# Weight pieces of 1024 elements in place of 512 for the later experts, and tokens taken counted in one column

## The chip, the cores and the metric

The kernel runs on one core of one Trainium2 chip. The core has a matrix engine (PE; PEld is its weight load), a vector engine (DVE), a scalar engine (ACT), a general engine (POOL) and a queue engine (SP) that issues most transfers. Each engine works through its own instructions in order and waits on semaphores for the others. The metric is the time of one execution in microseconds (us); three runs of the kernel before give the median.

## The reference

A sparse attention feeds a mixture of experts in which each expert has a fixed number of places:

```python
scores = scale * np.matmul(q, k.transpose(0, 1, 3, 2))     # 8 batches, 8 heads, 576 positions, 64 wide
masks = ...                                                # 4 heads local, 4 heads strided, stride 32
attn = exp(scores - max) / sum
x = (attn @ v) as (N, D) = (4608, 512)

cap = N // E                                               # 4608 / 8 = 576
logits = x @ w_gate
order = np.argsort(-flat)                                  # all (token, expert) pairs, best first
for idx in order:
    tok, e = (int(idx) // E, int(idx) % E)
    if assigned[tok] >= 0 or counts[e] >= cap:
        continue
    assigned[tok] = e
    counts[e] += 1
for e in range(E):
    mask = assigned == e
    h = np.maximum(x[mask] @ w1[e], 0.0)                   # w1[e]: 512 x 1024
    out[mask] = h @ w2[e]                                  # w2[e]: 1024 x 512
```

The assignment is greedy over all pairs, so the experts fill up one after the other: the first to fill is the one whose 576th best token has the highest logit, and so on.

## The kernel before

The first third of the span is attention, which writes the tokens to a scratch in HBM and leaves the logits in `L` (128 partitions x 36 columns of tokens x 8 experts). Then come eight phases (`ph`, called expert 0 to 7 here, in the order in which they fill up).

For each phase a *search* finds the threshold at which the next expert is full: six rounds, each with `cm` on DVE (L824, compares every token's best logit with 32 candidates), nine counting matmuls on PE (L840), `red` and `r` on DVE (L843, L846), a folding matmul (L849), `g` on DVE (L856 or L853), a spreading matmul (L859) and the next candidates `cand` (L862). `slots` numbers the chosen tokens (DVE and one pair of matmuls), `close` sets the filled expert's logits to a large negative number and finds every token's new best expert (`point`), `take` removes the chosen tokens, `indices` and `tokens` make the token list and gather the tokens. `ffn` does the expert's matmuls: `hidden` (L1159, x times w1, evacuated by ACT at L1166 and DVE at L1167) and the second product (L1207, L1201), stored at L1218.

Everything of float32 precision goes through PE as two float16 parts. `weights` fetches a phase's w1 and w2 (eight transfers on SP), squares them on ACT (`square`, L1002, four pieces of 1024 columns) to find a power of two as scale (`scale`, a matmul at L1010 and four small DVE instructions), and then cuts them: `split` writes `hi` = float16 of w times scale on ACT (L1020) and `lo` = the rest on DVE (L1021). `parts` says into which pieces: w1 (4 chunks x 1024 columns) into eight pieces of 4 x 128 columns, w2 (8 chunks x 512) into eight pieces of one chunk, each 512 elements in a partition.

PE's order is written out by hand from first to last (the generators yield a cost for each matmul, and the chain that is due next gets its turn); its matmuls for the search stand in fixed places between those of `ffn`. In phase 0 ACT's order is by hand as well. The order of the other engines comes from a planner that puts instructions into the order of their planned starts; work of the search and the evacuations is marked urgent, the pieces of the weights are not. `spread` hands the pieces over with due times (`T_SQ`, `T_SCALE`, `T_CUT`, 1500 each, after `T_W` of 4000), all at once when the phase that needs them has begun. So the search, its DVE work and the cutting of the next expert's weights run beside the matmuls of the present expert. The weights in float32 have one buffer (`wp`), hi and lo have two (`w16`).

`take` (L931) makes `pen`, a large negative number for each token taken, adds it to the tokens' best logits `rm`, and gives back a function that adds it to all eight logits of the token in `L`; the next search calls that function in its first round (`more`, L834).

Of the kernel before, what the change touches and what calls it, by code (L numbers as in the profile page):

```python
# [8 lines left out]
F32 = mybir.dt.float32  # L9
# [4 lines left out]
OP = mybir.AluOpType  # L14
# [5 lines left out]
N, DM, E, FF = B * S, H * D, 8, 1024  # L20
CAP = N // E
# [16 lines left out]
BIG = 1.0e30  # L38
J1, R1, GC = 32, 6, 4
J0, JL, R0, CUTS0 = 32, 16, 6, (16, 12, 8)  # L40
TP = 128
NC = N // TP
# [13 lines left out]
T_F, T_LOAD0, T_HOT1, T_W, T_SQ, T_SCALE, T_CUT, T_BULK0 = 3000, 1500, 6350, 4000, 1500, 1500, 1500, 600  # L56
# [76 lines left out]
def band_stride_attention_then_capacity_moe(ctx, tc, qt, kl, ks, nl, ns, wg, w1, w2, cst, out, dbg=None):  # L133
    nc = tc.nc
# [46 lines left out]
    L = const.tile([TP, NC, E], F32, name="L")  # L181
# [38 lines left out]
    with tc.tile_pool(name="ld", bufs=2) as ld, \  # L220
# [44 lines left out]
        class Unit:  # L265
# [71 lines left out]
            def room(u, p):  # L337
                u.sp[p] = ps_a.tile([128, 2, BANK], F32, name="spa")
# [133 lines left out]
        parts = (range(4, LT), range(4))  # L472
# [53 lines left out]
        todo = [Unit(b, strided) for b in range(B) for strided in (True, False)]  # L526
# [53 lines left out]
        def pair(i):  # L580
            return (todo[i // 2], i % 2) if 0 <= i <= last else None
# [27 lines left out]
        for i in range(-1, 2 * nu):  # L609
            u, n, m = pair(i), pair(i + 1), pair(i + 2)  # L610
# [7 lines left out]
            if m or i in mids:  # L618
                a = room(m) if m else ps_a.tile([128, 2, 512], F32, name="spa")
            if i in mids or i in mids2 or i in mids3:  # L620
                b = ps_b.tile([128, 512], F32, name="spb")
# [81 lines left out]
    rt = ctx.enter_context(tc.tile_pool(name="rt", bufs=2))  # L703
    r1 = ctx.enter_context(tc.tile_pool(name="r1", bufs=1))
# [28 lines left out]
                                       op1=OP.add)  # L733

    HV = 32
    rvb = [r1.tile([TP, HV, NC], F16, name=f"rv{i}") for i in range(2)]
    for t in rvb:
        nc.gpsimd.memset(t[:, 3 * SHI:], 0.0)
# [5 lines left out]
    def urgent(ph=1):  # L744
        return tc.high_priority(offset=URGENT * (2 if ph == 0 else 1))
# [183 lines left out]
            *point(slice(0, NC), rm, ohc, wmc)]  # L929

    def take(slot, rm):  # L931
        pen = rt.tile([TP, NC], F32, name="pen")
        nc.vector.tensor_scalar(pen, slot, CAP - 0.5, -BIG, op0=OP.is_lt, op1=OP.mult)
        nc.vector.tensor_tensor(rm, rm, pen, op=OP.add)
        return lambda: nc.vector.tensor_tensor(L, L, pen[:, :, None].to_broadcast([TP, NC, E]), op=OP.add)

    def indices(ph, slot):
        hurry = ph in HURRY
# [20 lines left out]
        with urgent(ph):  # L959
            pi = ps_r.tile([128, 512], F32, name="pr_")  # L960
            for c in range(NC):
                g = c % 4
                nc.tensor.matmul(pi[HV * g:HV * g + HV, :SLO], rv[:, :, c], ohl[c // nh][:, :, c % nh], start=(c < 4),
                                 stop=(c >= NC - 4), skip_group_check=True)
# [13 lines left out]
    def weights(ph, ei):  # L978
        e = nc.sync.value_load(ei[0:1, 0:1], min_val=0, max_val=E - 1)
        res, todo = [], []  # L980
        for name, w, nch, width, bits in (("w1", w1, DC, FF, W1_BITS), ("w2", w2, FC, DM, W2_BITS)):
            wf = wp.tile([128, nch, width], F32, name=name)
            src = w[bass.ds(e, 1)].rearrange("o (c p) f -> p (o c) f", p=128)
            n4 = nch // 4
            def fetch_w(cs, wf=wf, src=src, n4=n4):
                for c in cs:
                    nc.sync.dma_start(wf[:, c * n4:c * n4 + n4], src[:, c * n4:c * n4 + n4])  # L987

            k = W_EARLY if ph == 0 and name == "w2" else 4
            fetch_w(range(k))  # L990
            if k < 4:
                def later(wf=wf, k=k, n4=n4, go=fetch_w):
                    nc.gpsimd.memset(wf[:, k * n4:, :1], 0.0)
                    go(range(k, 4))
            sq = rt.tile([128, 4], F32, name="sq")
            sc = rt.tile([128, 2], I32, name="w_s" + name)
            hi = w16.tile([128, nch, width], F16, name=name + "h")
            lo = w16.tile([128, nch, width], F16, name=name + "l")

            def square(c, wf=wf, sq=sq, n4=n4):  # L1000
                jk = r1.tile([128, 1024], F16, name="jk")
                nc.scalar.activation(jk, wf[:, c * n4:(c + 1) * n4].rearrange("p c f -> p (c f)"), AF.Square,  # L1002
                                     scale=1.41422, accum_out=sq[:, c:c + 1])

            def scale(sq=sq, sc=sc, bits=bits):
                ss = rt.tile([128, 1], BF16, name="ss")
                with nc.allow_low_precision(reason="only the power of two of the sum is used, with a factor of two to spare"):
                    nc.vector.tensor_reduce(ss, sq, axis=AX.X, op=OP.add)
                pt = ps_r.tile([128, 512], F32, name="pr_")
                nc.tensor.matmul(pt[:, :1], ones_b, ss, start=True, stop=True)  # L1010
                scale_of(pt[:, :1], bits, rt, sc)

            def parts(nch=nch, width=width):
                if nch == DC:
                    return [(slice(0, nch), slice(k, k + 128)) for k in range(0, width, 128)]
                return [(slice(k, k + 1), slice(0, width)) for k in range(nch)]

            def split(c, f, k, wf=wf, sc=sc, hi=hi, lo=lo):
                s_ = sc.bitcast(F32)[:, 0:1]
                nc.scalar.activation(hi[:, c, f], wf[:, c, f], AF.Copy, scale=s_)  # L1020
                nc.vector.scalar_tensor_tensor(lo[:, c, f], wf[:, c, f], s_, hi[:, c, f], op0=OP.mult,  # L1021
                                               op1=OP.subtract)

            todo.append([(T_SQ, lambda c=c, g=square: g(c)) for c in range(4)])
            todo.append([(T_SCALE, scale)])
            todo.append([(T_CUT, lambda c=c, f=f, k=k, g=split: g(c, f, k)) for k, (c, f) in enumerate(parts())])
            res += [hi, lo, sc.bitcast(F32)]
        sq1, sc1, cut1, sq2, sc2, cut2 = todo
        if ph == 0:
            with urgent(0):  # L1030
                for _, f in sq1:
                    f()

            def start():
                return lambda: [f() for _, f in sc1]

            def more():
                with urgent(0):
                    for _, f in cut1[:CUT0]:
                        f()  # L1040
                g = spread(ph, cut1[CUT0:])
                chains.append([due_now(), g])
                second.append(slowly([(T_W20, lambda: None)] + sq2 + sc2 + cut2))
                chains.append([due_now(), second[0]])
                return g

            return res, (start, more, later)
        todo = [(T_W, lambda: None)] + sq1 + sc1
        for a, b in zip(cut1[:4], sq2):
            todo += [a, b]  # L1050
        todo += cut1[4:6] + sc2 + cut1[6:] + cut2
        g = spread(ph, todo)
        chains.append([due_now(), g])
        return res, g
# [178 lines left out]
    def due_now():  # L1233
        return clock
# [10 lines left out]
    with tc.manual_schedule(engines=MAN):  # L1245
        work[0] = now[:4] + (now[4](),)
        chains.append([T_LOAD0, load0()])
        for ph in range(E):
            with tc.manual_schedule(engines=MAN0) if ph in MANP else nullcontext():
                while ph not in ready:  # L1250
                    c = min(chains, key=lambda c: c[0])
# [79 lines left out]
```

## Time and profile before

| | us |
|---|---|
| median of 3 runs | 712.11 (708.58 to 715.13) |
| the profiled execution | 713.84 |
| its span, first to last instruction | 712.1 |
| expert 0 starts (first L1159) | 259.2 |
| last matmul of expert 7 | 700.8 |
| mean granted TensorE clock | 0.907 |

The span is the time between the first and the last instruction that the profiler saw; some 1.7 us of the execution lie around it. In the rows of the profile, a name such as `w2l<-w,w_sw,w2h` is what the instruction writes and reads, `128x512` is partitions x elements, and a bracket at the end of a timeline row is the idle time of the engine just before, with the one that ended it. A matmul's own time (some 0.38 us for 512 columns) overlaps the next one's. Groups of lines with the weight pieces: L1020 and L1021, 64 instructions each for w1 and w2, eight for each matrix.

### The profile page before, as it was taken

The numbers are of one execution on the slowest core, as the hardware profiler recorded it, in microseconds if no ns is written. First come the engines' busy times: TensorE is split into PE (matmuls) and PEld (weight loads), VectorE is DVE, ScalarE is ACT, GpSimd is POOL, SyncE is SP. The second block draws the span as 40 slices with busy tenths as digits, with TensorE's granted clock in tenths as the row PEclk, the third lists the DMA queues.
The fourth block names the chain that finished last, engine by engine and source line by source line (L and its number), as shares of the span: only waits on it lengthen the run. The fifth ranks groups of instructions, "written<-read, shape, count | busy, mean of one in ns | idle before, by whom it ended". The sixth has DMA issues, their size and how long they took to land.

```text
span 712.1 us, 19031 instructions
## 1 busy us (share of the span) xinstructions
PE 614.3 (86%) x7974; PEld 392.3 (55%) x7977; DVE 465.3 (65%) x1326; ACT 318.9 (45%) x497; POOL 156.7 (22%) x152
## 2 busy tenths in 40 slices
PE   7778777788984368899989999999999989999993
PEld 4555555566663346546635745745654754755741
DVE  4797656787786788858857877867768543552200
ACT  3635634554521055555544644833823746452210
POOL 2053413323331030050041031211212111402011
PEclk9888978987786579999999999999999999999997
DMA  9999999999642270391671671852652684341010
GB/s 252 265 262 255 248 230 255 239 234 209 167 103 67 68 231 28 135 267 36 237 156 45 238 154 46 276 110 90 229 112 75 237 236 151 90 94 52 2 37 29
DMA packets 111472, 111.24 MB, mean 156 GB/s; under 512 B 76405, under 2 KB 84175, under 8 KB 110876
## 3 DMA queue, kind: packets, MB, share of 16 engines
q1 hardware_dynamic: 103307, 88.49, 47.9%
q0 software_dynamic: 7360, 21.15, 9.5%
q8 instruction: 62, 1.02, 0.6%
q10 hardware_dynamic: 720, 0.39, 0.2%
q14 instruction: 23, 0.18, 0.1%
HBM read 73.63 MB, written 18.87 MB: 130 GB/s over the span
## 4 chain that ended last, share of the span: by engine, by line
PE 26%; issue 12%; DVE 10%; DMA 8%; ACT 3%; POOL 2%; SPq 1%; POOLq 0%; ACTq 0%
PE ph L1207 12%; PE ph L1159 8%; DMA w<-in_w_dram 7%; PE ph L1201 2%; DVE w2l L1021 2%; ACT jk L1002 2%; DVE cm L824 1%; POOL out_dram L1218 1%; DVE hl L1167 1%; SPq L987 1%; DVE w1l L1021 1%; DMA xg<-x_scr,idx 1%; POOL xg L1072 1%; ACT hh L1166 1%; DVE ohl L955 1%
## 5 line engine op out<-in xcount | busy, mean ns | idle before, releaser
L1159 PE MATMUL ph<-xt,w1h 128*128 128x288 f16 (+2 forms) x1024 | 177.5, 287 | 2.0 <-ACT xt L1062 2.0
L1159 PEld LDWEIGHTS <-w1h 128*128 128x128 f16 x1024 | 97.4, 98 | 30.9 <-issue 5.3
L1159 PE MATMUL ph<-xt,w1l 128*128 128x288 f16 (+2 forms) x512 | 111.4, 287 | 0.0
L1218 POOL DMA_INDIRECT out_dram<-y,idx x40 | 44.0, 1100 | 254.4 <-ACT y L1217 229.1
L1207 PE MATMUL ph<-w2l,hh 128*128 128x512 f16 x256 | 97.8, 382 | 2.3 <-DVE w2l L1021 2.3
L1207 PE MATMUL ph<-w2h,hh 128*128 128x512 f16 x256 | 97.9, 382 | 1.9 <-ACT hh L1166 1.9
L1002 ACT ACTIVATE jk<-w 128x1024 f16<-128x1024 f32 x64 | 67.4, 1053 | 71.3 <-DMA w<-in_w_dram 69.8
L1207 PE MATMUL ph<-w2h,hl 128*128 128x512 f16 x256 | 97.8, 382 | 0.2 <-DVE hl L1167 0.2
L1167 DVE SCALAR_TENSOR_TENSOR hl<-ph,hh 128x576 f16<-128x576 f32 (+2 forms) x72 | 49.3, 686 | 53.6 <-ACT hh L1166 53.4
L1207 PEld LDWEIGHTS <-hh 128*128 128x128 f16 x512 | 47.9, 98 | 56.6 <-issue 5.1
L1166 ACT ACTIVATE hh<-ph 128x576 f16<-128x576 f32 (+2 forms) x72 | 42.5, 591 | 79.8 <-PE ph L1159 78.4
L1072 POOL DMA_INDIRECT xg<-x_scr,idx x40 | 43.2, 1080 | 135.5 <-DVE idx L975 100.5
L380 ACT ACTIVATE pr<-spa 128x576 f32<-128x576 f32 x32 | 20.8, 649 | 92.8 <-PE spa L376 83.3
L1217 ACT ACTIVATE y<-ph,so 128x512 f32<-128x512 f32 x32 | 21.9, 685 | 89.5 <-PE ph L1207 79.9
L1159 PEld LDWEIGHTS <-w1l 128*128 128x128 f16 x512 | 49.5, 98 | 14.1 <-issue 2.3
L428 POOL TENSOR_TENSOR xos<-xs,xos 118x768 f16<-118x768 f32 x16 | 27.1, 1694 | 113.4 <-ACT xos L427 113.4
L1021 DVE SCALAR_TENSOR_TENSOR w1l<-w,w_sw,w1h 128x512 f16<-128x512 f32 x64 | 46.1, 743 | 2.4 <-ACT w1h L1020 1.6
L1021 DVE SCALAR_TENSOR_TENSOR w2l<-w,w_sw,w2h 128x512 f16<-128x512 f32 x64 | 45.8, 743 | 1.7 <-ACT w2h L1020 1.6
L397 PE MATMUL po<-v_s,pr 64*54 64x65 f32 (+1 forms) x768 | 41.3, 259 | 5.3 <-issue 3.8
L1020 ACT ACTIVATE w1h<-w,w_sw 128x512 f16<-128x512 f32 x64 | 41.6, 711 | 8.4 <-DVE g L856 3.7
L1020 ACT ACTIVATE w2h<-w,w_sw 128x512 f16<-128x512 f32 x64 | 41.0, 710 | 5.0 <-DVE w_sw L208 4.9
L1207 PEld LDWEIGHTS <-hl 128*128 128x128 f16 x256 | 25.1, 98 | 30.2 <-issue 3.1
(571 smaller groups left out, 947.2 us busy)
## 6 DMA issues: line engine op xcount, KB each, us to landing
w<-in_w_dram SPq DMA_DIRECT2D x64, 512.0 KB
kl<-in_kl_dram SPq DMA_DIRECT2D x16, 304.0 KB
v_s<-in_ns_dram SPq DMA_DIRECT2D x16, 292.5 KB
v_l<-in_nl_dram SPq DMA_DIRECT2D x16, 292.5 KB
ks<-in_ks_dram SPq DMA_DIRECT2D x16, 288.0 KB
qs<-in_qt_dram SPq DMA_DIRECT2D x16, 288.0 KB
ql<-in_qt_dram SPq DMA_DIRECT2D x16, 288.0 KB
x_scr<-xol SPq DMA_DIRECT2D x8, 512.0 KB
```

What stands on the lines that cost most here:

```text
L397: nc.tensor.matmul(po[r:r + n, j - j0], pr[k, o:o + n], u.vn[k, t, 2 * p + h], start=(j == j0), stop=(j == j1 - 1), skip_group_check=True)
L428: eng.tensor_tensor(u.xo[:nr, :, 1, c], xf, u.xo[:nr, :, 0, c], op=OP.subtract)
L1002: nc.scalar.activation(jk, wf[:, c * n4:(c + 1) * n4].rearrange("p c f -> p (c f)"), AF.Square, scale=1.41422, accum_out=sq[:, c:c + 1])
L1020: nc.scalar.activation(hi[:, c, f], wf[:, c, f], AF.Copy, scale=s_)
L1021: nc.vector.scalar_tensor_tensor(lo[:, c, f], wf[:, c, f], s_, hi[:, c, f], op0=OP.mult, op1=OP.subtract)
L1072: nc.gpsimd.indirect_dma_start(out=xg[:n], out_offset=None, in_=x_rows, in_offset=bass.IndirectOffsetOnAxis(ap=idx[:n, t:t + 1], axis=0))
L1159: nc.tensor.matmul(tile_[:, j, :w], wt[:, d, f * 128:(f + 1) * 128], xt[:, d // 2, xx, d % 2, c], start=(k == 0), stop=(k == 3 * DC - 1))
L1166: nc.scalar.activation(hv, src, AF.Relu)
L1167: nc.vector.scalar_tensor_tensor(lv, src, 0.0, hv, op0=OP.max, op1=OP.subtract)
L1207: nc.tensor.matmul(py, a[:, f, ts_], w[:, f], start=(k == 0), stop=(k == len(todo) - 1))
L1217: nc.scalar.activation(y, py, AF.Copy, scale=so[:, t:t + 1])
L1218: st = nc.gpsimd.indirect_dma_start(out=out_rows, out_offset=bass.IndirectOffsetOnAxis(ap=idx[:n, t:t + 1], axis=0), in_=y[:n], in_offset= ...
```

## The change

Two edits. In `weights`, `parts` makes pieces of twice the size for every phase but 0: w1 in four pieces of 4 x 256 columns, w2 in four pieces of two chunks, each 1024 elements in a partition; the due time of a piece is doubled with it. The list in which squares, scale and cuts follow one another is written anew for that: one cut of w1 ahead of each of the first three squares of w2, then the fourth square and the scale, then the last cut of w1 and those of w2.

In `take`, the tokens taken are counted in a column `taken` (one number for each token, zero at first), and `rm` gets `taken` times the large negative number. `L` is left alone: the function that was given back does nothing. Where `close` makes `rm` anew from `L`, the next `take` marks all tokens taken so far, not only the last ones.

```diff
+    taken = r1.tile([TP, NC], F32, name="taken")
+    nc.gpsimd.memset(taken, 0.0)
...
     def take(slot, rm):
-        pen = rt.tile([TP, NC], F32, name="pen")
-        nc.vector.tensor_scalar(pen, slot, CAP - 0.5, -BIG, op0=OP.is_lt, op1=OP.mult)
-        nc.vector.tensor_tensor(rm, rm, pen, op=OP.add)
-        return lambda: nc.vector.tensor_tensor(L, L, pen[:, :, None].to_broadcast([TP, NC, E]), op=OP.add)
+        nc.vector.scalar_tensor_tensor(taken, slot, CAP - 0.5, taken, op0=OP.is_lt, op1=OP.add)
+        nc.vector.scalar_tensor_tensor(rm, taken, -BIG, rm, op0=OP.mult, op1=OP.add)
+        return lambda: None
...
             def parts(nch=nch, width=width):
+                n = 2 if ph else 1
                 if nch == DC:
-                    return [(slice(0, nch), slice(k, k + 128)) for k in range(0, width, 128)]
-                return [(slice(k, k + 1), slice(0, width)) for k in range(nch)]
+                    return [(slice(0, nch), slice(k, k + 128 * n)) for k in range(0, width, 128 * n)]
+                return [(slice(k, k + n), slice(0, width)) for k in range(0, nch, n)]
...
-            todo.append([(T_CUT, lambda c=c, f=f, k=k, g=split: g(c, f, k)) for k, (c, f) in enumerate(parts())])
+            todo.append([(T_CUT * (2 if ph else 1), lambda c=c, f=f, k=k, g=split: g(c, f, k)) for k, (c, f) in enumerate(parts())])
...
         todo = [(T_W, lambda: None)] + sq1 + sc1
-        for a, b in zip(cut1[:4], sq2):
-            todo += [a, b]
-        todo += cut1[4:6] + sc2 + cut1[6:] + cut2
+        for k, a in enumerate(cut1[:3]):
+            todo += [a, sq2[k]]
+        todo += sq2[3:] + sc2 + cut1[3:] + cut2
```

## The prediction

> **What bounds the kernel now.** I read the page's head first, then the windows cut at the starts of the experts, then who waited for whom on PE, and last the timelines of DVE, ACT and PE around the weight pieces.
>
> ```profile
> span 712.1 us, 19031 instructions
> PE 614.3 (86%) x7974; PEld 392.3 (55%) x7977; DVE 465.3 (65%) x1326; ACT 318.9 (45%) x497; POOL 156.7 (22%) x152
> ```
>
> The windows show experts 1, 4 and 7 (columns: stretch, length, then busy time of PE, PEld, DVE, ACT, POOL, granted clock, DMA).
>
> ```profile
> 324.20:383.60 59.40, 55.79 (x433) 32.55 (x431) 44.95 (x130) 31.76 (x53) 10.75 (x10) 0.97 0.47 131
> ...
> 494.90:551.90 57.00, 53.95 (x422) 32.14 (x421) 42.25 (x133) 27.30 (x45) 11.91 (x10) 1.00 0.48 146
> ...
> 653.60:700.90 47.30, 47.19 (x313) 29.26 (x311) 6.81 (x9) 8.71 (x14) 4.80 (x5) 1.00 0.07 26
> ```
>
> Expert 7 has nothing beside it and takes 47.30 us, PE busy in 47.19: that is the matmul work of one expert. Experts 1 to 4 take 55 to 59 us. What they have more is the search for the next expert's threshold (its matmuls on PE) and stalls of PE. So PE sets the end, and the change touches no PE instruction of any size. ACT (27.30 of 57.00 us in expert 4) has room, DVE (42.25) some. The pieces can only move the time through the waits of PE. These are the ones after the first expert's start that matter (waits: waiter, whom for, us in total, times, longest):
>
> ```profile
> PE ph L1207 <- DVE w2l L1021: 2.3, 1, 2.3
> ...
> PE ph L1207 <- ACT hh L1166: 1.9, 1, 1.9
> PE pr__5641 L849 <- DVE r L846: 1.9, 1, 1.9
> ...
> PE pr__7713 L849 <- DVE red L843: 1.6, 1, 1.6
> ...
> PE pr__7012 L849 <- issue: 1.5, 1, 1.5
> ...
> PE pr__6336 L849 <- issue: 0.7, 1, 0.7
> ```
>
> and, asked of L849 alone, the waits of PE before it that r ended (us, times):
>
> ```profile
>   DVE r L846: 3.0, 5
> ```
>
> L849 is the second PE step of a search round (L840 counts, DVE makes red and r, L849 folds, DVE makes g, L859 spreads, DVE makes cand and cm, L840 again). PE's order is written out by hand, so when r is late, every matmul of the expert behind L849 waits. The four large L849 waits (1.9, 1.6, 1.5, 0.7) make 5.7 us.
>
> **Pieces of 1024.** For experts 1 to 7 each weight matrix is cut in 4 pairs of instructions (hi on ACT, lo on DVE) where it was 8: 56 pairs fewer in all. The durations:
>
> ```profile
> L1002 ACT ACTIVATE jk<-w 128x1024 f16<-128x1024 f32 x64 | 67.4, 1053 | 71.3 <-DMA w<-in_w_dram 69.8 <-ACT jk L1002 0.3
> ...
> L1021 DVE SCALAR_TENSOR_TENSOR w2l<-w,w_sw,w2h 128x512 f16<-128x512 f32 x64 | 45.8, 743 | 1.7 <-ACT w2h L1020 1.6
> ```
>
> The stretch that I replay is the second matrix of the expert prepared during expert 3, on ACT, DVE and PE:
>
> ```profile
> 479.75 4.40 ACT L1020 ACTIVATE w2h<-w,w_sw 128x512 f16<-128x512 f32 x7 [1.36 <-DVE w_sw L208]
> ```
>
> ```profile
> 480.17 1.36 DVE L824 TENSOR_TENSOR cm<-rmn,cand 128x1152 f16<-128x1152 f32 x1
> 481.44 2.07 DVE L1021 SCALAR_TENSOR_TENSOR w2l<-w,w_sw,w2h 128x512 f16<-128x512 f32 x3
> 483.43 0.18 DVE L843 TENSOR_TENSOR red<-pr__7241,fold 128x32 f16<-128x32 f32 x1
> 483.53 0.74 DVE L1021 SCALAR_TENSOR_TENSOR w2l<-w,w_sw,w2h 128x512 f16<-128x512 f32 x1
> 484.19 0.20 DVE L846 TENSOR_REDUCE r<-red 128x8 f16<-128x32 f16 x1
> ...
> 486.38 0.20 DVE L862 SCALAR_TENSOR_TENSOR cand<-steps,pr__7241,cand 128x1 f32<-128x1 f32 x1
> 486.51 0.73 DVE L1021 SCALAR_TENSOR_TENSOR w2l<-w,w_sw,w2h 128x512 f16<-128x512 f32 x1
> ...
> 487.46 1.34 DVE L824 TENSOR_TENSOR cm<-rml,steps 128x1152 f16<-128x1152 f32 x1
> ```
>
> ```profile
> 482.80 0.38 PE L840 MATMUL pr__7241<-ohn,cm 128*128 128x32 f16 x9
> 484.63 0.18 PE L849 MATMUL pr__7241<-r,fold 128*32 128x8 f16 x1
> 486.14 0.17 PE L859 MATMUL pr__7241<-ih,ones_j 32*128 32x1 f16 x1
> 489.28 0.38 PE L840 MATMUL pr__7309<-ohn,cm 128*128 128x32 f16 x9
> ```
>
> On ACT seven pieces take 4.40 us, 0.63 apiece. A 1024 square takes 1.05, less some 0.09 of overlap with the next (0.71 alone against 0.63 in the train), so 0.96: each merged pair saves 2 x 0.63 - 0.96 = 0.30, over 56 pairs 17 us of ACT time. On DVE three take 2.07, so one more costs 0.67. The nearest long row is cm, 1152 elements in 1.36 alone and 1.27 to the next start (480.17 to 481.44): scaled to 1024 some 1.15 to 1.20. I take 1.20, a saving of 2 x 0.67 - 1.20 = 0.14, 8 us in all. Neither is on the path: ACT idles half the stage, and DVE's weights are ready well ahead (this matrix is done at 487, and the expert that uses it starts at 494.9). So: 0 us.
>
> What is on the path is that DVE does not interrupt a piece. Between red (483.43) and r (484.19) a piece was put into the gap that r waits for red, and another ran into red's start. I replay with 1.20: the hi pieces are ready at 480.8, 481.8, 482.7, 483.7; DVE runs one from 481.44 to 482.64 and one to 483.84, so red starts at 483.84 and not 483.43. A third fills the gap from 483.95 to 485.15, r ends at 485.35, and L849 starts near 485.4 in place of 484.63: 0.8 us of new stall. The fourth ends at 486.47, ahead of L859 at 486.14 + 0.8, so it costs nothing. One matrix pays 0.8 once. Searches run while experts 0 to 4 compute, so ten matrices (two each of experts 1 to 5) meet one. For the five second matrices I take 0.8 each; the five first ones have squares of 1.05 us between their pieces on ACT, so they reach DVE less densely, and I take half: 5 x 0.8 + 5 x 0.4 = 6. From that goes what small pieces cost there now: r ended five waits of 3.0 us in all, and without the 1.9 four are left with 1.1, one of them beside expert 0's own pieces; I take 0.8. Sum **+5.2**. The ends: 0, if the planner keeps the gaps free, less the 0.8; and 1.4 a matrix, +13, if a piece also lands ahead of cand and between cand and cm. That link has 0.5 us of room (cm ends at 487.46 + 1.34 = 488.80, PE takes it at 489.28), and two places at 1.20 - 0.67 = 0.53 each are 1.1, so 0.6 more.
>
> **Stops of DVE that no engine explains.** Three of the four L849 waits follow idle time on DVE before red, although L840 had ended long before:
>
> ```profile
> 364.18 0.19 DVE L843 TENSOR_TENSOR red<-pr__5641,fold 128x32 f16<-128x32 f32 x1 [2.53 <-PE ph L1201]
> ...
> 463.43 0.19 DVE L843 TENSOR_TENSOR red<-pr__7012,fold 128x32 f16<-128x32 f32 x1 [0.94 <-PE ph L1159]
> ...
> 517.60 0.19 DVE L843 TENSOR_TENSOR red<-pr__7713,fold 128x32 f16<-128x32 f32 x1 [1.08 <-PE ph L1159]
> ```
>
> ```profile
> 364.18:412.72 48.54, 38.67 (x114) 1.00 0.48 142
> 412.72:463.43 50.71, 38.37 (x114) 1.00 0.54 160
> 463.43:517.60 54.17, 38.71 (x115) 1.00 0.49 142
> ```
>
> ```profile
> q14 instruction: 23, 0.18, 0.1%
> ```
>
> The stops lie 114 or 115 counted DVE instructions apart (busy instructions of the windows that begin and end at them), as a fixed block of the instruction stream would, and the instruction queue loads 0.18 MB in 23 packets, 8 KB each. My reading is that DVE waits for its next block of instructions, once an expert, each time just before red. The change takes 9 DVE instructions out of each later expert (8 pieces, 1 update of L), so the stops wander off red by 9, 18, 27 places. Where a stop lands outside a search round it costs PE nothing, inside one about as much as now. These three waits are 5.0 us; I take **-2**, ends 0 and -5.0.
> The Trainium skill, page "Runtime: NRT & Kernel Launch", section "Instruction fetch mechanics", says that a sequencer fetches its next block while it runs the present one, so that the crossing is mostly hidden. The idle 2.53, 0.94 and 1.08 us speak against that for DVE. By the page's rule this term would be 0 and the sum 2 us higher.
>
> **Tokens taken.**
>
> ```profile
> 444.18 0.19 DVE L900 SCALAR_TENSOR_TENSOR sc<-df,mine 128x36 f16<-128x36 f32 x1
> ...
> 448.08 0.18 DVE L933 TENSOR_SCALAR pen<-slot 128x36 f32<-128x36 f32 x1
> ...
> 448.29 0.20 DVE L934 TENSOR_TENSOR rmn<-rmn,pen 128x36 f32<-128x36 f32 x1
> 448.41 0.45 DVE L935 TENSOR_TENSOR L<-L,pen 128x288 f32<-128x288 f32 x1
> ```
>
> Two instructions stay two, now both of the kind of L900 (0.19, an upper end of 0.26 for f32 output): +0.1 at most, seven times, in a stretch where PE has other matmuls. Six updates of L of 0.45 go (0.37 each to the next start at 448.78). Only the one late in expert 0 can be on the path: PE waits 2.3 us there for w2l, whose last piece is queued on DVE behind the work on the next expert's tokens: **-0.4**, ends 0 and -2.3 (if the planner also moves that piece ahead). The memset of 36 columns is one more on POOL, which is busy 22% of the span: 0. In the new order of the todo list only ACT squares and the scale of the second matrix change places with cuts; the due times add up as before (28000 to the scale, 43000 to the end), no DMA is moved, and SP's and POOL's queues stay: 0.
>
> **One wait absorbs.** L1207 waits 1.9 us for hh on ACT late in expert 5, where ACT is held by squares that wait for weights from HBM. PE coming later loses that much less: **-0.9**, ends 0 and -1.9.
>
> **Sum.** 5.2 - 2 - 0.4 - 0.9 = +1.9 us. The profiled execution took 713.84 us (span 712.1 and 1.7 around it), 0.2% above the median 712.11. Against it the sum gives 715.7, against the median **714**.
>
> **The rivals.** *Slower.* Every one of the ten matrices pays in both links, 1.4 us: +13 in place of 5.2, sum +9.9, **722 us**. It decides from about 1.1 us a matrix (7.1 us for the 1%, and 3.3 + 0.8 to make up, over ten). For it: the gaps between red and r and between cand and cm are filled with pieces wherever pieces are there. Against: with half as many pieces, a matrix rarely has one for each gap. *Faster.* The planner leaves no long piece in a gap (0 - 0.8), all three stops leave search rounds (-5.0) and the w2l wait goes (-2.3), with 0.7 of the fourth L849 wait: **703 us**. Against: search rounds fill most of each expert's time, so a stop finds another one. *Hidden.* New stalls equal what the stops and the 0.4 give: **712 us**, if only the second matrices pay 0.8 (4 - 0.8 - 2 - 0.4 - 0.9 = 0).
>
> **How the numbers follow.** Forecast 714 (and its surroundings above 712) 0.35, hidden 0.23, slower 0.25, faster 0.17. A time within 1% of 712.11 (705.0 to 719.2) is what a measurement of this kernel can't tell from no change: 0.58 for that, 0.25 above it, 0.17 below. The range 704 to 724 leaves out about half of the faster case and the edge of the slower one.
>
> **What would show it.** L1020 and L1021 rows of 128x1024 x56 and near 0.96 and 1.2 us; DVE's count 62 lower. Right on the main step: L849 and L840 waits on r and cm of 0.3 to 1 us in several rounds of experts 0 to 4, a 1024 piece between red and r. Wrong if those rounds keep their 1.8 us from L840 to L849. Right on the stops: long idle time of DVE without a late releaser, off red and off the places above. If it is still before red in each expert, the block reading is wrong. The prediction as a whole is wrong if PE's waits in experts 5 to 7 or before 255 us change by more than 2 us.

## The result and the profile after

| | before | after |
|---|---|---|
| median of 4 runs each (us) | 713.55 (708.58 to 715.13) | 721.81 (720.62 to 724.61) |
| ratio, 95% interval | 1 | 1.0107 [1.0062, 1.0152] |
| the profiled execution (us) | 713.84 | 722.52 |
| its span (us) | 712.1 | 720.8 |
| mean granted TensorE clock | 0.907 | 0.902 |
| expert 0 starts, expert 7 ends (us) | 259.2, 700.8 | 260.9, 709.6 |

By the ratio the kernel became slower by 1.1%, 7.6 us; the two medians lie 8.3 us apart. The head of the page after:

```profile
span 720.8 us, 18914 instructions
...
PE 619.2 (86%) x7974; PEld 396.1 (55%) x7977; DVE 457.3 (63%) x1264; ACT 308.5 (43%) x441; POOL 166.5 (23%) x153
```

DVE has 62 instructions less and is busy 8.0 us less, ACT 10.4 us less. Two engines do less, and the span is 8.7 us longer: what they save is not on the path, as the prediction had it.

The windows of the profiled kernel after show experts 2, 4, 5 and 7 (columns as in the prediction), and those of the kernel before experts 2 and 5, which the prediction did not show.

```profile
382.40:441.70 59.30, 55.51 (x424) 32.53 (x423) 42.52 (x115) 25.57 (x37) 13.25 (x10) 0.97 0.43 132
499.00:556.50 57.50, 53.98 (x422) 32.03 (x421) 41.06 (x123) 25.69 (x37) 15.07 (x10) 1.00 0.54 145
556.50:613.30 56.80, 51.19 (x355) 30.75 (x354) 22.48 (x52) 32.81 (x51) 13.03 (x10) 0.94 0.69 199
662.30:709.60 47.30, 47.18 (x313) 29.25 (x311) 6.81 (x9) 8.72 (x14) 4.79 (x5) 1.00 0.07 26
```

```profile
383.60:438.50 54.90, 53.91 (x424) 32.22 (x423) 44.39 (x126) 27.10 (x46) 11.42 (x10) 1.00 0.48 142
551.90:604.10 52.20, 49.60 (x356) 30.41 (x355) 23.55 (x60) 31.74 (x55) 9.01 (x9) 1.00 0.66 205
```

The lengths say where to look. Expert 7 is 47.30 us as before; expert 2 is 4.4 us longer and expert 5 4.6 us. Over all eight the gain and loss come to +7.0 us (441.6 to 448.6). The other 1.7 us lie ahead of the experts, where the change has one memset, and where the start moves from run to run in any case: over the traces of all kernels shown here expert 0 starts between 255.8 and 264.8 us.

The waits of PE after (waiter, whom for, us in total, times, longest; most lines are two higher here, so L849 is L851 now, L840 is L842, L1207 is L1209):

```profile
PE ph L1209 <- ACT hh L1168: 5.3, 1, 5.3
...
PE pr__6954 L851 <- DVE r L848: 2.2, 1, 2.2
...
PE pr__6296 L851 <- DVE r L848: 2.1, 1, 2.1
...
PE pr__7637 L851 <- DVE r L848: 1.7, 1, 1.7
...
PE pr__4952 L842 <- DVE cm L826: 1.2, 1, 1.2
...
PE pr__5619 L851 <- DVE r L848: 0.6, 1, 0.6
```

and asked of L851 alone, where the kernel before had five waits of 3.0 us:

```profile
  DVE r L848: 10.8, 11
```

So there are two places: the search (many waits for r, some for cm) and one single wait for hh, 1.9 us before and 5.3 now. The wait for w2l of 2.3 us is gone from the list.

Some waits stand in the profile as "issue", so for comparing kernels I worked the stalls out in one way for all: between the starts of two successive matmuls of PE, less the first one's own 0.12 or 0.21 us, summed where over 0.15 us is left, from the first L1159 on (L1161 after). By it:

| kernel | hi on ACT | lo on DVE | take | ratio to before [95%] | r | cm | hh | w2l | idx, tokens | experts |
|---|---|---|---|---|---|---|---|---|---|---|
| before | 512 | 512 | old | 1 | 8.6 | 2.8 | 2.1 | 2.4 | 7.6 | 441.6 |
| after | 1024 | 1024 | new | 1.0107 [1.0062, 1.0152] | 12.8 | 4.6 | 5.4 | 0 | 6.3 | 448.6 |
| e1 | 1024 | 1024 | old | 1.0187 [1.0129, 1.0245] | 12.9 | 4.6 | 6.5 | 2.4 | 8.8 | 455.7 |
| e2 | 512 | 512 | new | 0.9987 [0.9951, 1.0022] | 9.4 | 3.0 | 3.2 | 0 | 8.0 | 442.1 |
| e3 | 1024 | 512 | new | 0.9907 [0.9868, 0.9947] | 7.1 | 3.3 | 0 | 0 | 8.4 | 435.8 |
| e4 | 512 | 1024 | new | 1.0064 [1.0028, 1.0099] | 13.3 | 4.4 | 2.3 | 0 | 6.3 | 444.6 |
| e5 (after, gap closed) | 1024 | 1024 | new | 1.0018 [0.9979, 1.0056] | 4.5 | 5.6 | 5.7 | 0 | 6.8 | 443.0 |
| e6 (before, gap closed) | 512 | 512 | old | 1.0047 [1.0008, 1.0086] | 3.8 | 4.2 | 4.7 | 2.4 | 10.2 | 445.2 |
| e7 (e3, gap closed) | 1024 | 512 | new | 0.9939 [0.9897, 0.9980] | 3.9 | 5.2 | 0 | 0 | 8.1 | 435.3 |
| e8 (before, 64 more on DVE) | 512 | 512 | old | 1.0000 [0.9952, 1.0047] | 5.0 | 3.4 | 4.3 | 2.4 | 7.8 | 441.8 |
| e9 (after, hh first) | 1024 | 1024 | new | 1.0072 [1.0036, 1.0107] | 13.2 | 5.5 | 0 | 0 | 9.4 | 447.9 |
| e10 (e2, hh first) | 512 | 512 | new | 0.9957 [0.9921, 0.9993] | 7.5 | 3.3 | 0 | 0 | 9.5 | 438.9 |
| e11 (e5, hh first) | 1024 | 1024 | new | 0.9991 [0.9967, 1.0016] | 3.1 | 6.3 | 0 | 0 | 11.0 | 445.9 |
| e12 (e3 again) | 1024 | 512 | new | 0.9943 [0.9899, 0.9987] | 4.7 | 4.7 | 0 | 0 | 8.8 | 435.3 |

The stalls are those of one profiled execution each; the ratios leave out disturbed runs, which the medians given with the experiments still hold. How far two executions differ can be seen from e8, which is the kernel before but for 64 small instructions at its start and takes the same time: r and cm wait 8.4 us there in place of 11.4, hh 4.3 in place of 2.1. A difference of some 3 us in one column between two kernels is therefore no finding by itself. A wait for y on ACT, of 0.6 to 3.5 us in e9 to e12, has no column. From before to after r and cm together grow by 6.0 us, hh by 3.3, w2l goes by 2.4, idx and tokens by 1.3: +5.6 of the +7.0 us of the experts. All stalls together, the small ones too, grow by 6.7 us by the same count; the remaining 0.3 us I do not assign.

Now the same stretch that the prediction replayed (second matrix, prepared during expert 3). The timelines of ACT, DVE and PE after:

```profile
483.08 4.26 ACT L1022 ACTIVATE w2h<-w,w_sw 128x1024 f16<-128x1024 f32 x4 [1.37 <-DVE w_sw L208]
```

```profile
483.50 1.36 DVE L826 TENSOR_TENSOR cm<-rmn,cand 128x1152 f16<-128x1152 f32 x1
484.77 2.47 DVE L1023 SCALAR_TENSOR_TENSOR w2l<-w,w_sw,w2h 128x1024 f16<-128x1024 f32 x2
487.16 0.18 DVE L845 TENSOR_TENSOR red<-pr__7177,fold 128x32 f16<-128x32 f32 x1
487.26 1.28 DVE L1023 SCALAR_TENSOR_TENSOR w2l<-w,w_sw,w2h 128x1024 f16<-128x1024 f32 x1
488.46 0.20 DVE L848 TENSOR_REDUCE r<-red 128x8 f16<-128x32 f16 x1
...
490.42 0.22 DVE L864 SCALAR_TENSOR_TENSOR cand<-steps,pr__7177,cand 128x1 f32<-128x1 f32 x1 [0.35 <-PE pr__7177 L861]
```

```profile
486.13 0.38 PE L842 MATMUL pr__7177<-ohn,cm 128*128 128x32 f16 x9
488.71 0.17 PE L851 MATMUL pr__7177<-r,fold 128*32 128x8 f16 x1 [0.68 <-DVE r L848]
490.21 0.17 PE L861 MATMUL pr__7177<-ih,ones_j 32*128 32x1 f16 x1
```

Two long pieces run ahead of red, a third between red and r, and PE takes r 2.58 us after the start of its counting (486.13 to 488.71), where it was 1.83 (482.80 to 484.63). That is 0.75 us later; the replay had 0.8. The fourth piece ended early enough, as in the replay.

In the three rounds where DVE stood still before red in the kernel before, DVE does not stand still now. This is the second of them, DVE after:

```profile
463.49 2.48 DVE L1023 SCALAR_TENSOR_TENSOR w1l<-w,w_sw,w1h 128x1024 f16<-128x1024 f32 x2
465.88 0.75 DVE L1169 SCALAR_TENSOR_TENSOR hl<-ph,hh 128x576 f16<-128x576 f32 x1
466.54 0.18 DVE L845 TENSOR_TENSOR red<-pr__6954,fold 128x32 f16<-128x32 f32 x1
466.64 1.28 DVE L1023 SCALAR_TENSOR_TENSOR w1l<-w,w_sw,w1h 128x1024 f16<-128x1024 f32 x1
467.83 0.20 DVE L848 TENSOR_REDUCE r<-red 128x8 f16<-128x32 f16 x1
```

The stop is gone, and the wait that PE has for it is larger than before (2.2 in place of 1.5), because long pieces stand ahead of red and behind it. (The tile of this round is `pr__7012` in the kernel before.)

### The profile page after: what moved, and what is told of

Read it like the earlier page. It is cut to its first block, busy times and chain, and to the rows that moved or that the text cites. A ratio compares the mean times of both kernels' runs of the same rounds, so it can differ in the third digit from the quotient of the medians.

```text
span 720.8 us, 18914 instructions
## 1 busy us (share of the span) xinstructions
PE 619.2 (86%) x7974; PEld 396.1 (55%) x7977; DVE 457.3 (63%) x1264; ACT 308.5 (43%) x441; POOL 166.5 (23%) x153
## 4 chain that ended last, share of the span: by engine, by line
PE 23%; issue 17%; DVE 12%; DMA 8%; ACT 3%; POOL 3%; SPq 1%; POOLq 0%; DVEq 0%; ACTq 0%
PE ph L1209 12%; PE ph L1161 7%; DMA w<-in_w_dram 6%; DVE w1l L1023 2%; DVE w2l L1023 2%; PE ph L1203 2%; ACT jk L1003 2%; DVE cm L826 2%; DMA xg<-x_scr,idx 1%; POOL out_dram L1220 1%; DVE hl L1169 1%; POOL xg L1074 1%; SPq L988 1%; ACT hh L1168 0%; ACT w2h L1022 0%
## 5 line engine op out<-in xcount | busy, mean ns | idle before, releaser
L1161 PE MATMUL ph<-xt,w1h 128*128 128x288 f16 (+2 forms) x1024 | 177.9, 288 | 1.1 <-DVE w1l L1023 1.1
L1161 PEld LDWEIGHTS <-w1h 128*128 128x128 f16 x1024 | 97.6, 98 | 30.9 <-issue 5.3
L1161 PE MATMUL ph<-xt,w1l 128*128 128x288 f16 (+2 forms) x512 | 111.5, 288 | 0.0
L1220 POOL DMA_INDIRECT out_dram<-y,idx x40 | 48.8, 1221 | 250.7 <-ACT y L1219 227.2
L1209 PE MATMUL ph<-w2h,hh 128*128 128x512 f16 x256 | 98.0, 383 | 5.3 <-ACT hh L1168 5.3
L1209 PE MATMUL ph<-w2h,hl 128*128 128x512 f16 x256 | 98.1, 383 | 0.0
L1209 PE MATMUL ph<-w2l,hh 128*128 128x512 f16 x256 | 98.0, 383 | 0.0
L1209 PEld LDWEIGHTS <-hh 128*128 128x128 f16 x512 | 47.8, 98 | 62.8 <-issue 6.0
L1074 POOL DMA_INDIRECT xg<-x_scr,idx x40 | 47.5, 1189 | 136.2 <-DVE idx L976 86.9
L1161 PEld LDWEIGHTS <-w1l 128*128 128x128 f16 x512 | 49.5, 98 | 15.1 <-issue 3.3
L1023 DVE SCALAR_TENSOR_TENSOR w1l<-w,w_sw,w1h 128x1024 f16<-128x1024 f32 (+1 forms) x36 | 41.2, 1159 | 3.6 <-ACT w1h L1022 3.6
L1023 DVE SCALAR_TENSOR_TENSOR w2l<-w,w_sw,w2h 128x1024 f16<-128x1024 f32 (+1 forms) x36 | 41.3, 1158 | 2.9 <-ACT w2h L1022 2.8
L826 DVE TENSOR_TENSOR cm<-rmn,cand 128x1152 f16<-128x1152 f32 x30 | 40.7, 1356 | 0.6
L1209 PEld LDWEIGHTS <-hl 128*128 128x128 f16 x256 | 25.1, 98 | 28.6 <-issue 1.3
L397 PEld LDWEIGHTS po<-v_s,pr 64*54 64x54 f32 (+1 forms) x768 | 31.7, 149 | 14.4 <-issue 8.8
```

Source lines behind the costliest of these rows:

```text
L397: nc.tensor.matmul(po[r:r + n, j - j0], pr[k, o:o + n], u.vn[k, t, 2 * p + h], start=(j == j0), stop=(j == j1 - 1), skip_group_check=True)
L826: nc.vector.tensor_tensor(cm, src[:, :, None].to_broadcast([TP, NC, J1]), t[:, None, :].to_broadcast([TP, NC, J1]), op=OP.is_ge)
L1074: nc.gpsimd.indirect_dma_start(out=xg[:n], out_offset=None, in_=x_rows, in_offset=bass.IndirectOffsetOnAxis(ap=idx[:n, t:t + 1], axis=0))
L1161: nc.tensor.matmul(tile_[:, j, :w], wt[:, d, f * 128:(f + 1) * 128], xt[:, d // 2, xx, d % 2, c], start=(k == 0), stop=(k == 3 * DC - 1))
L1209: nc.tensor.matmul(py, a[:, f, ts_], w[:, f], start=(k == 0), stop=(k == len(todo) - 1))
L1220: st = nc.gpsimd.indirect_dma_start(out=out_rows, out_offset=bass.IndirectOffsetOnAxis(ap=idx[:n, t:t + 1], axis=0), in_=y[:n], in_offset= ...
```

## The experiments

**One edit at a time.** e1 has the pieces and the old `take`:

```diff
...
-                    return [(slice(0, nch), slice(k, k + 128)) for k in range(0, width, 128)]
-                return [(slice(k, k + 1), slice(0, width)) for k in range(nch)]
+                    return [(slice(0, nch), slice(k, k + 128 * n)) for k in range(0, width, 128 * n)]
+                return [(slice(k, k + n), slice(0, width)) for k in range(0, nch, n)]
```

> Pieces of 1024 for experts 1 to 7, take as before. Theory (a long DVE piece ahead of the search's red, r or cm makes PE wait): 6 to 9 us over the kernel before, and 8 or 9 of the waits of the folding matmul for r at 0.5 us or more. Rival (the edit of take costs the time): within 2 us of the kernel before.

Measured: 727.98 us beside 717.63 for the kernel before, ratio 1.0187 [1.0129, 1.0245], which is 9.3 to 17.6 us over: more than the 6 to 9 expected. r and cm wait as long as in after (17.5 us together), eight of the waits for r are of 0.5 us or more, and the 2.4 us for w2l are back.

e2 has the new `take` and pieces of 512:

```diff
...
-        nc.vector.tensor_tensor(rm, rm, pen, op=OP.add)
-        return lambda: nc.vector.tensor_tensor(L, L, pen[:, :, None].to_broadcast([TP, NC, E]), op=OP.add)
+        nc.vector.scalar_tensor_tensor(rm, taken, -BIG, rm, op0=OP.mult, op1=OP.add)
+        return lambda: None
```

> Only the edit of take. Theory: within 2 us of the kernel before, rather below (six updates of L of 0.45 us less on DVE, the order of the pieces unchanged). Rival (take costs the time): 4 us or more over the kernel before.

Measured: 0.9987 [0.9951, 1.0022], some 0.9 us below, within the 2 us expected. The edit of `take` does not cause the loss; the pieces do. The w2l wait is gone with the new `take` in all kernels that have it and stands at 2.4 us in all that lack it (before, e1, e6, e8); yet e2 is not faster by that, since hh waits 3.2 in place of 2.1 and r 9.4 in place of 8.6.

**Which of the two halves of a pair.** In e3 and e4 one half of each pair is long and the other short. e3 (hi 1024 on ACT, lo 512 on DVE; `two` gives the two halves of a piece):

```diff
...
-                nc.vector.scalar_tensor_tensor(lo[:, c, f], wf[:, c, f], s_, hi[:, c, f], op0=OP.mult,
-                                               op1=OP.subtract)
+                for a, b in two(c, f):
+                    nc.vector.scalar_tensor_tensor(lo[:, a, b], wf[:, a, b], s_, hi[:, a, b], op0=OP.mult,
+                                                   op1=OP.subtract)
```

> The changed kernel, but each lo piece on DVE cut in two of 512; hi on ACT stays 1024, and the order of squares, scale and cuts is the changed one. Theory (the length on DVE is what costs): within 2 us of the kernel before; waits of L849 for r no larger than before. Rival (the longer ACT pieces, or the new order of the list, hold up hh or the scale): 5 us or more over the kernel before, with the wait of PE for hh near 5 us.

Measured: 710.64 us, ratio 0.9907 [0.9868, 0.9947]: faster than both kernels, 3.8 to 9.5 us below the kernel before where at most 2 were expected. e4 is the reverse:

```diff
...
-                nc.scalar.activation(hi[:, c, f], wf[:, c, f], AF.Copy, scale=s_)
+                for a, b in two(c, f):
+                    nc.scalar.activation(hi[:, a, b], wf[:, a, b], AF.Copy, scale=s_)
```

> The changed kernel, but each hi piece on ACT cut in two of 512; lo on DVE stays 1024. Theory: 5 to 10 us over the kernel before, as the changed kernel. Rival (ACT's length): within 2 us of the kernel before.

Measured: 721.19 us, ratio 1.0064 [1.0028, 1.0099], 2.0 to 7.1 us over where 5 to 10 were expected. DVE of e3 in the stretch of the replay:

```profile
481.48 2.07 DVE L1033 SCALAR_TENSOR_TENSOR w2l<-w,w_sw,w2h 128x512 f16<-128x512 f32 x3
483.47 0.18 DVE L845 TENSOR_TENSOR red<-pr__7205,fold 128x32 f16<-128x32 f32 x1
483.57 0.74 DVE L1033 SCALAR_TENSOR_TENSOR w2l<-w,w_sw,w2h 128x512 f16<-128x512 f32 x1
484.23 0.20 DVE L848 TENSOR_REDUCE r<-red 128x8 f16<-128x32 f16 x1
```

r starts 0.76 us after red, as in the kernel before (0.76), and not 1.30 as in after. Through the whole kernel the picture is the same: r and cm wait 17.4 to 18.7 us where lo is 1024 (after, e1, e4, e9) and 8.4 to 12.4 where it is 512 (before, e2, e3, e8, e10, e12), whatever hi is; these are the kernels in which the gap between red and r is open. The length of the DVE half is the cause of the search's part.

**The gap between red and r.** In e5 the work that stood ahead of the counting matmuls (`pre`) is moved behind red, and the two rounds of each search that have none get an instruction of the same size, so that the planner has no gap there to fill with a piece:

```diff
...
+                        with tc.issue_after(rins.ins):
+                            nc.vector.tensor_scalar(pre, steps[:, rd + 1, :n], cand[:, 0:1], None, op0=OP.add)
+                if last or n == 1:
+                    with tc.issue_after(rins.ins):
+                        idle = rt.tile([128, J1 + 1], F32, name="idle")
+                        nc.vector.tensor_scalar(idle, steps[:, rd, :J1 + 1], cand[:, 0:1], None, op0=OP.add)
```

> The changed kernel, with pre (or a copy of its size, in the two rounds that have none) put between red and r, so that no lo piece stands there in any of the 36 rounds (9 pieces of 1024 stand there in the changed kernel). Theory (the piece in the gap is the larger part of the loss): r waits of PE fall from 12.8 us to 6 to 9, and the time is 1 to 5 us over the kernel before, in place of 8. Rival (the loss comes from long pieces that are under way when red, cand or hh become ready): r waits stay at 11 us or more, the time 6 us or more over the kernel before.

Measured: 717.75 beside 717.87, ratio 1.0018 [0.9979, 1.0056]. A round of e5 on DVE:

```profile
484.17 0.19 DVE L840 TENSOR_TENSOR red<-pr__7259,fold 128x32 f16<-128x32 f32 x1 [1.15 <-PE pr__7259 L837]
484.28 0.23 DVE L850 TENSOR_SCALAR idle<-steps 128x33 f32<-128x33 f32 x1
484.42 0.20 DVE L853 TENSOR_REDUCE r<-red 128x8 f16<-128x32 f16 x1
```

r follows red by 0.25 us, and r's waits fall from 12.8 to 4.5 us. With long pieces kept and only their place forbidden, most of the loss is gone: the gap is where they cost. (In DVE's order of the kernel after, a 1024 piece stands between red and r in 9 of 36 rounds, in expert 0's preparation a 512 one in 2 more; in e5 in none.)

e6 is the same edit on the kernel before.

> The kernel before, with the same filling of the gap between red and r (12 pieces of 512 of experts 1 to 5 stand there before). Theory: 0 to 3 us below the kernel before, since a piece of 512 costs the round only a few tenths; r waits from 8.6 us to 6 to 8. Rival: no change within 1 us.

Measured: 719.82, ratio 1.0047 [1.0008, 1.0086]. This was a miss: r falls by 4.8 us, and the kernel is slower by 0.5%. In its trace hh waits 2.6 us more, idx and tokens 2.6, cm 1.4: what the search gained was given back (of these, 2.2 for hh and 0.6 for cm are what e8 shows without the edit).

e7 is the same edit on e3.

> hi pieces of 1024 on ACT, lo pieces of 512 on DVE, the edit of take, and the gap between red and r filled. Theory: 7 to 10 us below the kernel before, at or a little below the version without the filling (6.6 below). Rival (filling costs DVE as much as it saves): 3 to 6 us below.

Measured: 713.89, ratio 0.9939 [0.9897, 0.9980], some 4.4 us below the kernel before, less than the 7 to 10 expected and what the rival had. It is nothing better than e3 without the filling (r less by 3.2, cm more by 1.9).

**The stops of DVE.** e8 puts 64 small instructions on DVE at the program's start. If the stops came every so many instructions, they would move by 64 places, half the distance between them.

```diff
+    pad = const.tile([128, 1], F32, name="pad")
+    for _ in range(64):
+        nc.vector.memset(pad, 0.0)
```

> The kernel before, with 64 one-column memsets on DVE at its start, so that every later DVE instruction stands 64 places further on. Theory (DVE stops once in some 128 of its instructions for the next block of them): the idle times of DVE before red at 364, 463 and 518 us are gone or stand at other instructions, about half a block away, and the r waits change by 2 us or more in sum; time from 4 us below to 2 us above the kernel before. Rival (red waits for something else there): the same three idle times of 1 to 2.5 us before red, time within 1 us.

Measured: 1.0000 [0.9952, 1.0047]. DVE of e8:

```profile
366.20 0.74 DVE L1024 SCALAR_TENSOR_TENSOR w1l<-w,w_sw,w1h 128x512 f16<-128x512 f32 x1
369.21 0.15 DVE L859 TENSOR_SCALAR_CACHE_REDUCE g<-pr__5706 32x8 f16<-32x8 f32 x1 [2.26 <-PE ph L1210]
...
466.91 0.19 DVE L846 TENSOR_TENSOR red<-pr__7077,fold 128x32 f16<-128x32 f32 x1 [0.92 <-PE ph L1162]
```

`pr__5706` and `pr__7077` are the tiles of the rounds in which the kernel before stopped (`pr__5641` and `pr__7012`: one tile and 64 instructions add 65 to the number). The stops stayed, 2.26 us before g and 0.92 before red, while 64 instructions had been put ahead of them. The third is not seen in this run. So they are not bound to a count of instructions.

The trace also holds the times at which semaphores are raised, and they say what DVE waited for: PE's signal that the counting matmuls are done. In the kernel before it comes 0.01 us after the recorded end of the last of them in 30 of the 36 rounds. In the three rounds with a stop it comes 2.44, 1.79 and 1.87 us after; for `pr__5641` the recorded end is 361.71, the signal 364.16 and the start of red 364.18. In e8 the signal of `pr__7077` comes at 466.89, 1.77 us after the recorded end, and red starts at 466.91. The bracket `<-PE` of these rows says the same: DVE did not lack instructions, and the end that the profile records for a matmul is modelled. In the kernel after, none of the 36 signals is late. In e9 below, which has the same pieces, that of `pr__6954` is late by 1.68 us, DVE runs long pieces meanwhile, and PE's wait for r is 2.2 us as in after. So the late signals differ from one execution to the next, and their absence in after can't be put down to the change. Why they are late is open.

The packets of the instruction queues, in the same two traces, did move: those that fall in with DVE's count came at 410.9, 461.6 and 514.8 us before and at 389.5, 437.4 and 489.4 in e8, and DVE of e8 has no such stop at those times. This is what the Trainium skill, page "Runtime: NRT & Kernel Launch", section "Instruction fetch mechanics", says, that crossing a block is mostly hidden; on this point the runs agree with the page and not with my prediction.

**The wait for hh.** ACT, after, around the wait of 5.3 us in expert 5:

```profile
579.34 0.65 ACT L1168 ACTIVATE hh<-ph 128x576 f16<-128x576 f32 x1 [1.80 <-PE ph L1161]
590.30 1.06 ACT L1003 ACTIVATE jk<-w 128x1024 f16<-128x1024 f32 x1 [10.31 <-DMA w<-in_w_dram]
...
591.36 0.63 ACT L1168 ACTIVATE hh<-ph 128x576 f16<-128x576 f32 x1
```

ACT's order has the first square of expert 7's weights ahead of the last hh of expert 5. The square waits 10.31 us for its weights, and the hh stands behind it. The order is the same in the kernel before, with a shorter wait:

```profile
582.74 1.06 ACT L1002 ACTIVATE jk<-w 128x1024 f16<-128x1024 f32 x1 [6.75 <-DMA w<-in_w_dram]
...
583.79 0.63 ACT L1166 ACTIVATE hh<-ph 128x576 f16<-128x576 f32 x1
```

In e3 the planner put the hh first, and nothing waits behind the square:

```profile
577.32 0.65 ACT L1178 ACTIVATE hh<-ph 128x576 f16<-128x576 f32 x1 [2.29 <-PE ph L1171]
582.51 1.06 ACT L1003 ACTIVATE jk<-w 128x1024 f16<-128x1024 f32 x1 [4.54 <-DMA w<-in_w_dram]
```

Why the weights come later is on SP's queue. SP before, then after:

```profile
570.20 8.30 SPq L1075 DMA_TRANSPOSE xt<-xg  x5
578.75 3.12 SPq L987 DMA_DIRECT2D w<-in_w_dram  x4
```

```profile
574.46 11.49 SPq L1077 DMA_TRANSPOSE xt<-xg  x5
586.22 1.96 SPq L988 DMA_DIRECT2D w<-in_w_dram  x4
```

The weights are issued behind the five transposes of the gathered tokens: 26.9 us after expert 5's start before (578.75 - 551.9), 29.7 after (586.22 - 556.5). These 2.9 us are near the 3.4 that hh waits longer. The transposes took 8.30 and 11.49 us; from the start of the first gather to that of the last transpose it is 10.4 us before, 12.6 in e8, 10.2 in e3, 10.3 in e4, 13.4 after, 14.9 in e1 and 15.7 in e11. The short ones include e4, with long lo pieces, so their length alone does not set it, and e8 has the pieces of the kernel before; what does is open. With e8's 4.3 us for hh it is open, too, how much of the 3.3 us belongs to the change.

To take the wait away, e9 holds expert 7's squares until the last hh of expert 5, on the kernel after:

```diff
...
+                with tc.issue_after(last_hh[(E - 1) * FC - 1]) if ph == E - 1 else nullcontext():
+                    nc.scalar.activation(jk, wf[:, c * n4:(c + 1) * n4].rearrange("p c f -> p (c f)"), AF.Square,
+                                         scale=1.41422, accum_out=sq[:, c:c + 1])
```

> The changed kernel; on ACT the squares of expert 7's weights are put behind the last hh of expert 5 (in the changed kernel the first square, which waits for its transfer, stands ahead of that hh, and PE waits 5.3 us for it). Theory (this wait is a second place that gives some of the loss, apart from the long lo pieces): the wait of L1207 for hh is gone, the r and cm waits stay at about 17 us, and the time is 2 to 5 us over the kernel before, in place of 8. Rival (PE waits as long elsewhere for the same transfers): 6 to 9 us over.

Measured: 723.75 beside 717.13, ratio 1.0072 [1.0036, 1.0107], 2.6 to 7.7 us over, between and across the two expectations. hh no longer waits; y, on ACT behind the same squares, makes PE wait 1.8 us, and the waits for idx and tokens are 9.4 where they were 6.3. Its interval overlaps that of after, so a gain from it is not shown.

e10 is the same order on e2.

> Pieces of 512 on both engines, the edit of take, and the squares of expert 7 behind the last hh of expert 5. Theory (the version with hi 1024 and lo 512 owed its 6.6 us mostly to that order, which the planner fell into, and to the wait for w2l that the edit of take removes): 4 to 8 us below the kernel before, as the version with hi 1024 and lo 512. Rival (hi pieces of 1024 on ACT gave it): within 2 us of the kernel before.

Measured: 713.59, ratio 0.9957 [0.9921, 0.9993], 0.5 to 5.7 us below. The interval reaches from less than the expected gain into it: undecided in size, faster than before.

e9 and e10 are the cleanest pair for the pieces: both have the new `take` and no wait for hh, and they differ in the pieces and their list. Their ratios, 1.0072 and 0.9957, have intervals that lie apart, by some 8 us, and r and cm wait 18.7 and 10.8 us, 7.9 apart.

e11 has both edits on the kernel after, the gap closed and hh first.

> The changed kernel with the gap between red and r filled and with expert 7's squares behind the last hh of expert 5. Theory (the two places add up): both the r waits (under 6 us) and the hh wait (0) are small, time 3 to 7 us below the kernel before, with pieces of 1024 on both engines. Rival (one absorbs the other): within 2 us of the version with the filling alone (1.3 us over the kernel before).

Measured: 717.04, ratio 0.9991 [0.9967, 1.0016]. A miss; the rival had it. Both waits are small or gone (r 3.1, hh 0), and the time does not differ from that of e5 beyond the intervals. PE waits elsewhere:

```profile
PE ph L1216 <- ACT y L1226: 3.2, 1, 3.2
```

and 11.0 us for idx and tokens against 6.8 in e5. The two gains do not add up. The two profiled executions are no fair pair for the lengths, though: that of e5 (713.23) was the fastest of its twelve runs and that of e11 (722.23) the slowest.

**The best version again.** e12 is e3 once more, measured later.

> The version with hi 1024 on ACT, lo 512 on DVE and the edit of take once more, beside the kernel before on the chip of this call. Theory (short lo pieces keep the r and cm waits at 10 to 12 us, and neither PE's wait for w2l nor the one for hh is there): 4 to 8 us below the kernel before, no wait of L1207 for hh. Rival (the first measurement of it was a lucky one): within 2 us.

Measured: 710.90 beside 721.04, ratio 0.9943 [0.9899, 0.9987]. It is faster than the kernel before in both measurements, by 0.9% and 0.6%. Whether the long hi pieces give that, or the order into which the planner falls with them (the last hh ahead of the squares), is not settled: e10 has that order with pieces of 512, and its interval overlaps with both.

## Why the prediction was partly right

The time, 721.8 us, lies in the range 704 to 724, and the direction of the sum (+1.9) was right; the likeliest value, 714, was 8 us too low, and what came is the time of the rival called slower (722), though not in its way. That the range of 20 us holds is partly luck: the terms were off by +2.8, -2.0, +4.2 and -1.3 us, which cancel in part, and the pieces with the old `take`, for which the same terms give 5.2 - 2 - 0.9 = +2.3, cost 13.4 us in e1.

**The long pieces in the search: right in mechanism, too small in size.** The replay foretold 0.8 us for the round that it followed, and 0.75 was measured; pieces stand in the gap once in nine of the ten matrices. e3 against the kernel after shows the length of the DVE half as the cause of the waits, e5 the gap as the place. The term was +5.2; e9 against e10 puts the pieces at some 8 us. One page of the Trainium skill, "Perfetto Trace Analysis", section "Optimizing Scalar/DVE Operations", says that where Vector is not saturated and makes others idle, breaking up instructions may let work be done sooner. That is this case: DVE is busy 63% of the span, PE waits 10.8 us for r at L851, and e3, with lo broken up, is faster. The prediction did not weigh that rule.

**The stops of DVE, -2: the step that failed in its reading.** It took 114 counted instructions between stops for a block of the instruction stream, and took the matmuls for done at their recorded ends. e8 shows that the stops stay when the count is shifted, and the signals show DVE waiting for PE. That they are not seen in after freed next to nothing: the time was taken by long pieces ahead of red and behind it. The three rounds with a stop, which cost 1.9, 1.5 and 1.6 us, now cost 0.6, 2.2 and 1.7 (the waits of `pr__5619`, `pr__6954`, `pr__7637`), and that of expert 2, 0.7 before, costs 2.1 (`pr__6296`). The prediction summed the pieces and the stops as though they were apart, +5.2 - 2 = +3.2; r and cm together grew by 6.0.

**The wait for hh, -0.9: wrong in sign.** The reasoning was that PE comes later and the weights do not. But the weights are fetched behind transposes, which wait for gathers, which wait for the search's result (idx): when the experts run late, the transfer is as late. Expert 5 started 4.6 us later in after, and the weights were issued 7.5 us later. The wait grew by 3.4 in the two traces; e8, with no change of time, has 2.2 more than before, so the size of this term is not settled. With the stops this is what the likeliest value lacked. The prediction's last clause, that it would be wrong as a whole if waits in experts 5 to 7 changed by more than 2 us, is met by this wait.

**Tokens taken, -0.4: wrong in size.** The wait for w2l is gone to the last 2.3 us, the low end given: without the update of L the planner places that last piece ahead of the next search's cm. e2 shows that little of it reaches the end with pieces of 512. With those of 1024 the ratio of after is 0.8% below that of e1, but their intervals overlap, so a gain from the edit is not shown.

**The rest.** The 1024 pieces take 1.28 us alone on DVE and 1.20 in the train (estimate 1.20), and 1.05 on ACT in the train (estimate 0.96: too low, at no cost to the sum):

```profile
L1023 DVE SCALAR_TENSOR_TENSOR w2l<-w,w_sw,w2h 128x1024 f16<-128x1024 f32 x28 | 35.3, 1276 | 2.8 <-ACT w2h L1022 2.8
...
L1022 ACT ACTIVATE w2h<-w,w_sw 128x1024 f16<-128x1024 f32 x28 | 30.3, 1138 | 3.9 <-DVE w_sw L208 3.8
```

That both engines' savings lie beside other work was right.

By term, in us: search (pieces and stops) +3.2 foretold and +6.0 measured; w2l -0.4 and -2.4; hh -0.9 and +3.3; idx and tokens not foretold and -1.3.

## What to carry to other kernels

A piece of background work can delay a short chain on the same engine by its whole length. Where PE waits for such a chain, merging the pieces saves time that nobody waits for and lengthens the chain, so leave them short on the engine where it runs (here DVE). Long pieces on the engine that the chain does not use (here ACT) did no harm in e3; that they gain anything is not shown. When a wait is removed, look for the next place that is bound to a transfer or a gather and ask whether its due time moves along: in e6 4.8 us gained at r, and in e11 5.7 gained at hh, were taken back in other waits. A pattern in distances (114, 114, 115) is a hypothesis that one run with a shifted count can test, before it is put into a sum; where a row names a releaser whose work seems long done, the time at which its semaphore was raised tells whether the engine waited for it.

## What the runs showed of the hardware

PE's signal that a group of matmuls is done came 1.8 to 2.4 us after the recorded end of the group in three of the 36 rounds of the kernel before, where 0.01 us is usual, and DVE stood still for 0.9 to 2.5 us for it; in e8 two of these rounds have a late signal again although DVE's instruction count had moved. At these times POOL issues its indirect transfers; POOL of e8, ahead of the stop that ends at 369.21, and of the one that ends at 466.91:

```profile
365.86 1.10 POOL L1075 DMA_INDIRECT xg<-x_scr,idx  x1 [0.30 <-issue]
367.26 1.00 POOL L1221 DMA_INDIRECT out_dram<-y,idx  x1 [0.30 <-issue]
```

```profile
464.98 1.17 POOL L1075 DMA_INDIRECT xg<-x_scr,idx  x1 [0.30 <-issue]
466.45 0.90 POOL L1075 DMA_INDIRECT xg<-x_scr,idx  x1 [0.30 <-issue]
```

That one causes the other was not tried, and other issues of POOL go by without a stop; the cause stays open. The chain from the first gather to the last transpose of that expert took between 10.2 and 15.7 us for the same work, a spread of 5.5 us beside the 7.6 that were measured here.
